# More unread products in TensorE's waits of the first routing, and the first expert's rows ahead of the second routing on VectorE

## The chip, the cores and the metric

The kernel runs on one core of one Trainium2 chip. Its engines run side by side: TensorE multiplies matrices (PE in the profile; PEld is its weight load), VectorE (DVE) and ScalarE (ACT) work element by element, GpSimd (POOL) does small vector work and issues the gathers and scatters, SyncE (SP) issues most other transfers. The metric is the time of one execution on the device in microseconds (us), the median of several runs; lower is better.

## The reference

`x` is the output of an attention layer (a local one and one over means of four positions), 4608 tokens of 512 numbers. Then eight experts share the tokens, each with room for exactly 576:

```python
logits = x @ w_gate                       # 4608 x 8
order = np.argsort(-logits.flatten())     # the best pairs (token, expert) first
for idx in order:
    tok, e = idx // 8, idx % 8
    if assigned[tok] >= 0 or counts[e] >= 576: continue
    assigned[tok] = e; counts[e] += 1
for e in range(8):
    mask = assigned == e
    out[mask] = np.maximum(x[mask] @ w1[e], 0) @ w2[e]   # 512 -> 1024 -> 512
```

## The kernel before, in words

A first part computes attention and the logits (tile `lg`). The second part has eight rounds, one for each expert in the order in which experts fill up.

**Routing (class Routing).** A round finds which expert is full first and at which logit. It looks for the threshold digit by digit, in two halves of the logit's bits (high, then low), three steps each: VectorE compares all keys with a row of thresholds (`cmp`, L802), TensorE counts the hits per expert (L839), VectorE caps the counts (`cs`, L843), TensorE adds them up (L847), VectorE finds the step that is passed (`un`, L854), TensorE hands it to all partitions (L864, L865), and VectorE makes the next thresholds (`thr`, L826). Every step waits for the other engine. Then `emit` ranks the chosen tokens (L1090, L1091) and turns ranks into a list of token numbers, `idx` (one-hot tiles `ohh`, `ohl`, a product of both at L1131, or L1167 in round 0).

**Unread products.** In round 0 TensorE has nothing else to do. `fill(what)` then issues FILL[what] products of a tile of ones (128x256, L789) into a bank `pX` that nobody reads; `rows` does the same with XFILL (L1304) while it waits for the first gathered rows. They stand in TensorE's order like any instruction, ahead of what follows.

**Experts (class Experts).** `weights` loads a round's weights, and `split` cuts each into two fp16 halves, `wh` on ScalarE (L1262) and `wl` on VectorE (L1267, two pieces each). `gather` fetches the token rows (five slices `xg`, GpSimd, L1290). `rows` of round 0 transposes a slice on TensorE (L1313, bank `pX`, two buffers), and ScalarE (L1316) and VectorE (L1318) write its high and low halves to `xt`: these are the row halves of the title. `first` is the first layer, 192 products a round (L1358), which needs slices 0 and 1 for its first columns and 2 to 4 for the rest; `relu` evicts it on ScalarE and VectorE (`ht`, L1386, L1390); `second` is the second layer (L1413, 120 products); `store` scatters the result.

**The order.** Engines execute in the order in which the program issues. Each of these streams has a name and a round, and the table KEYS gives every step of a stream a number; `Plan.run` always issues the step with the smallest number. S is the setup of a routing, R its search and `emit`, W `split`, X `rows`, H `first`, E `relu`, C `second`, L and M the weight loads, G `gather`, Y `store`. S1 and R1 are thus the second routing, which runs beside the layers of the first expert (H0, C0).

Of the kernel before, what the change touches and what calls it, by code (L numbers as in the profile page):

```python
# [6 lines left out]
F32 = mybir.dt.float32  # L7
# [24 lines left out]
NT = NTOK // 128  # L32
# [668 lines left out]
FILL = {"oh": 8, "level": 5, "low": 5, "row": 3, "tot": 4, "rank": 2, "list": 11, "half": 0}  # L701
XFILL = (22, 5, 8)
# [19 lines left out]
class Routing:  # L722
# [37 lines left out]
    def open(self, ctx, ps, ident):  # L760
# [6 lines left out]
        self.zeros = wk.tile([128, 2 * NT], F32, name="zeros")  # L767
        nc.vector.memset(self.zeros, 0.0)
        self.id16 = wk.tile([128, 224], F16, name="id16")
        nc.vector.memset(self.id16[:, 128:], 0.0)  # L770
# [10 lines left out]
        nc.gpsimd.memset(self.ohl[:, NT:], 0.0)  # L781
        nc.scalar.dma_start(self.tri, consts["tri"])
# [33 lines left out]
    def count(self, oh, key, cmp, cap, first, beside=None, tell=None):  # L816
# [5 lines left out]
        for lv, (J, step) in enumerate(LV):  # L822
# [14 lines left out]
            for t in range(0, NT, n):  # L837
                m = min(n, NT - t)
                nc.tensor.matmul(cv[:m * J, :, :m], cmp[:, t:t + m].rearrange("p t j -> p (t j)"), oh[:, :, t:t + m],  # L839
                                 start=t == 0, stop=t + m == NT, skip_group_check=True)  # L840
            yield
# [369 lines left out]
class Experts:  # L1211
# [905 lines left out]
```

## Time and profile before

| what | value |
|---|---|
| median of 3 runs | 707.5 us (703.14, 707.5, 708.33) |
| the profiled execution | 702.79 us |
| its span, first to last instruction | 701.2 us |
| mean granted TensorE clock | 0.972 |

The profile is of one execution; what it has beside its span is 1.6 us. A line of a timeline gives start, duration, engine, source line, operation and names, and in brackets the idle time of the engine just before and what ended it. A granted clock of 1.00 is 2.4 GHz, of 0.50 it is 1.2 GHz.

### The profile page before, as it was taken

Reading aid. Unit: us, or ns where it says so; the run is one execution under the profiler, and the core shown is the slowest. Engines: PE = TensorE matmul, PEld = TensorE weight load, DVE = VectorE, ACT = ScalarE, POOL = GpSimd, SP = SyncE. Lnnn points to the kernel's source line nnn. Section 1 sums busy time; section 2 is a strip of 40 time slices with the busy share of each in tenths; the row PEclk is TensorE's granted clock in tenths of the full one; section 3 lists DMA queues with packets and bytes.
Section 4 is the critical chain, followed back from the end, with each engine's and each line's share of the span. In section 5 each row is a group of like instructions: output and inputs, shape, how many; then the busy total and the mean of one; then the engine's idle time right before and its main releaser. Section 6 shows DMA issues by size and latency. Waiting matters only on the chain.

```text
span 701.2 us, 19377 instructions
## 1 busy us (share of the span) xinstructions
PE 655.7 (94%) x7871; PEld 471.2 (67%) x7871; DVE 485.1 (69%) x1311; ACT 358.0 (51%) x712; POOL 259.5 (37%) x322
## 2 busy tenths in 40 slices
PE   7799989999899878899999899999999999999994
PEld 4678878888888856674675576576574664764741
DVE  5778585778678867799997897896896775510300
ACT  5787977988786723335344453352542454412210
POOL 7678747584684214005131141411501405002011
PEclk9999999999999966999999999999999999999997
DMA  8959888776886615337483661942833976101001
GB/s 241 309 145 234 210 243 245 212 230 197 208 239 181 212 59 180 129 128 230 103 292 101 233 158 44 315 102 70 314 68 123 393 167 164 40 1 62 9 31 38
DMA packets 137714, 116.77 MB, mean 167 GB/s; under 512 B 86232, under 2 KB 114392, under 8 KB 137624
## 3 DMA queue, kind: packets, MB, share of 16 engines
q1 hardware_dynamic: 130104, 93.71, 46.3%
q0 software_dynamic: 6512, 21.24, 9.2%
q8 instruction: 62, 1.02, 0.6%
q10 hardware_dynamic: 1008, 0.58, 0.3%
q14 instruction: 28, 0.23, 0.1%
HBM read 86.00 MB, written 21.23 MB: 153 GB/s over the span
## 4 chain that ended last, share of the span: by engine, by line
PE 46%; DVE 20%; issue 19%; ACT 7%; DMA 4%; POOL 2%; SPq 0%; POOLq 0%; DVEq 0%; ACTq 0%
PE pX L1413 15%; PE pH L1358 12%; PE o L569 3%; DVE wl L1267 2%; PE g L511 2%; POOL out_dram L1437 2%; DVE gtmp L266 2%; PE g L546 2%; PE pR L839 1%; ACT pt L554 1%; DVE ht L1390 1%; PE g L599 1%; DVE cmp L802 1%; PE g L300 1%; DMA nat<-in_q_dram 1%
## 5 line engine op out<-in xcount | busy, mean ns | idle before, releaser
L1358 PE MATMUL pH<-xt,wh 128*128 128x256 f16 (+1 forms) x1024 | 191.0, 286 | 2.6 <-DVE ht L1390 1.9
L1413 PE MATMUL pX<-wh,ht 128*128 128x512 f16 (+1 forms) x640 | 183.0, 379 | 0.0
L1358 PE MATMUL pH<-xt,wl 128*128 128x320 f16 (+1 forms) x512 | 144.7, 287 | 0.0
L1413 PEld LDWEIGHTS <-ht 128*128 128x128 f16 (+1 forms) x960 | 81.6, 100 | 87.3 <-issue 3.0
L1437 POOL DMA_INDIRECT out_dram<-y,idx x40 | 43.8, 1094 | 217.0 <-ACT y L1432 200.0
L1413 PE MATMUL pX<-wl,ht 128*128 128x512 f16 (+1 forms) x320 | 117.9, 380 | 0.0
L1358 PEld LDWEIGHTS <-wh 128*128 128x128 f16 x1024 | 94.6, 98 | 29.1 <-DVE ht L1390 3.0
L1386 ACT ACTIVATE ht<-pH 128x512 f16<-128x512 f32 (+1 forms) x128 | 45.5, 407 | 116.3 <-PE pH L1358 103.1
L1390 DVE SCALAR_TENSOR_TENSOR ht<-pH,ht 128x512 f16<-128x512 f32 (+1 forms) x128 | 52.3, 450 | 60.2 <-ACT ht L1386 60.1
L1267 DVE SCALAR_TENSOR_TENSOR wl<-nat,wh 128x512 f16<-128x512 f32 x128 | 86.7, 686 | 4.5 <-ACT wh L1262 3.9
L1290 POOL DMA_INDIRECT xg<-x_dram,idx x40 | 48.0, 1201 | 72.0 <-DVE idx L1144 37.2
L1432 ACT ACTIVATE y<-pX 128x512 f32<-128x512 f32 (+2 forms) x41 | 23.9, 584 | 93.9 <-PE pX L1413 56.5
L1262 ACT ACTIVATE wh<-nat 128x1024 f16<-128x1024 f32 x64 | 67.0, 1056 | 8.1 <-DMA nat<-in_moe_w_dram 7.3
L1358 PEld LDWEIGHTS <-wl 128*128 128x128 f16 x512 | 50.1, 98 | 12.8
L554 ACT COPY pt<-g 38x512 f32<-38x512 f32 x72 | 41.7, 579 | 17.4 <-PE g L546 15.0
L569 PE MATMUL o<-vw,pt 128*64 128x64 f32 x1152 | 41.6, 224 | 1.8 <-DMA vw<-up_dram 1.7
L536 POOL TENSOR_TENSOR sw<-sw,rs 128x304 f32<-128x304 f32 x36 | 26.3, 734 | 43.1 <-DVE rs L534 24.1
L511 PE MATMUL g<-kt,qz 128*64 128x38 f32 x1152 | 41.1, 225 | 1.1 <-ACT kt L279 1.1
L300 PE MATMUL g<-ident,nat 128*128 128x128 f32 x256 | 37.3, 279 | 4.6 <-DMA nat<-in_k_dram 1.3
L511 PEld LDWEIGHTS g<-kt,qz 128*64 128x64 f32 x1152 | 40.1, 138 | 1.7 <-ACT kt L279 1.2
L569 PEld LDWEIGHTS o<-vw,pt 128*64 128x64 f32 x1152 | 37.1, 138 | 3.9 <-ACT x L581 1.8
L266 POOL TENSOR_TENSOR gtmp<-qz 64x576 f32<-64x576 f32 x28 | 32.0, 1141 | 11.9 <-ACT qz L279 4.2
(227 smaller groups left out, 1135.6 us busy)
## 6 DMA issues: line engine op xcount, KB each, us to landing
nat<-in_moe_w_dram SPq DMA_DIRECT2D x28, 1024.0 KB
vw<-in_v_dram SPq DMA_DIRECT2D x136, 78.0 KB
x_dram<-x SPq DMA_DIRECT2D x36, 256.0 KB
nat<-in_q_dram SPq DMA_DIRECT2D x7, 1024.0 KB
nat<-in_k_dram SPq DMA_DIRECT2D x7, 1024.0 KB
nat<-in_v_dram SPq DMA_DIRECT2D x7, 1024.0 KB
vw<-up_dram SPq DMA_DIRECT2D x36, 64.0 KB
up_dram<-xu SPq DMA_DIRECT2D x8, 256.0 KB
```

The costliest lines, as they stand in the source:

```text
L266: eng.tensor_tensor(tmp.rearrange("p a (w i) -> p a w i", w=NW) if which == "q" else tmp, sv[..., ::2], sv[..., 1::2], op=OP.add)
L511: nc.tensor.matmul(sv[64 * a:64 * a + 64, 4 * g + c], self.qz[b % 2][:, 2 * g + a, w].rearrange("p s q -> p (s q)"), self.kt[b][:, 2 * g + ...
L554: nc.scalar.copy(out[r, :, :, a], p[r].rearrange("p (i h q) -> p i h q", h=4, q=QW))
L569: nc.tensor.matmul(o[64 * i:64 * i + 64, 64 * (4 * g + h):64 * (4 * g + h) + 64], pt[:, 2 * g + i, h].rearrange("p b q -> p (b q)"), self. ...
L1262: nc.scalar.activation(hi, r, AF.Copy, scale=sc)
L1267: nc.vector.scalar_tensor_tensor(lo[:, a:a + LOP], r[:, a:a + LOP], sc, hi[:, a:a + LOP], op0=OP.mult, op1=OP.subtract)
L1290: self.fetched = self.nc.gpsimd.indirect_dma_start(out=xg[:n], out_offset=None, in_=self.x, in_offset=bass.IndirectOffsetOnAxis(ap=idx[:n, ...
L1358: nc.tensor.matmul(p[:, s, :s1 - s0], self.w[k, d][a][:, 128 * f:128 * f + 128], self.xt[k][:, b, d, s0:s1], start=j == 0, stop=j == len(s ...
L1386: nc.scalar.activation(hi, q, AF.Relu)
L1390: nc.vector.scalar_tensor_tensor(lo, q, 0.0, hi, op0=OP.max, op1=OP.subtract)
L1413: nc.tensor.matmul(p[o:o + m], self.ht[k][:, f, h0:h0 + m], self.w[k, 4 + f // 2][b][:, 512 * (f % 2):512 * (f % 2) + 512], start=j < part ...
L1437: i = nc.gpsimd.indirect_dma_start(out=self.out, in_=y[:n], in_offset=None, out_offset=bass.IndirectOffsetOnAxis(ap=plan.vals["idx", k][:n ...
```

## The change

FILL and XFILL are larger, there is one more place with unread products ("kept", four of them, behind the first count of the low half), two tiles are cleared on GpSimd instead of VectorE (`zeros` also later and at another address), and the numbers of rounds 0 and 1 in KEYS are new. All names of an engine's order below come from the program itself; line numbers of the changed kernel are two higher from L843 on.

```diff
-FILL = {"oh": 8, "level": 5, "low": 5, "row": 3, "tot": 4, "rank": 2, "list": 11, "half": 0}
-XFILL = (22, 5, 8)
+FILL = {"oh": 18, "level": 8, "low": 7, "kept": 4, "row": 3, "tot": 4, "rank": 2, "list": 18, "half": 0}
+XFILL = (32, 6, 8)
...
-        self.zeros = wk.tile([128, 2 * NT], F32, name="zeros")
-        nc.vector.memset(self.zeros, 0.0)
         self.id16 = wk.tile([128, 224], F16, name="id16")
-        nc.vector.memset(self.id16[:, 128:], 0.0)
+        nc.gpsimd.memset(self.id16[:, 128:], 0.0)
...
+        self.zeros = wk.tile([128, 2 * NT], F32, name="zeros")
+        nc.gpsimd.memset(self.zeros, 0.0)
...
+            if beside and not lv:
+                self.fill("kept")
...
-    "X0": [70, 72, 76, 77, 80, 82, 83, 85, 89, 90, 93, 97, 100, 102, 105, 106],
+    "X0": [69, 70, 71, 73, 75, 76, 79, 80, 81, 84, 85, 86, 92, 93, 94, 95],
```

On VectorE, between the token list of round 0 and the first capped count of the second routing, before (`eq`, `u`, `am`, `amu`, `oh` and the two big `cmp` are S1; the numbers in names are of tiles):

```order
L1267 SCALAR_TENSOR_TENSOR wl_5257<-nat,wh_5256 128x512
L1318 SCALAR_TENSOR_TENSOR xt<-pX,xt 128x4x128
L948 TENSOR_REDUCE am<-eq 128x36
L950 SCALAR_TENSOR_TENSOR amu<-asg,am 128x36
L951 TENSOR_TENSOR oh<-eq,amu 128x288
L1318 SCALAR_TENSOR_TENSOR xt<-pX,xt 128x4x128
L802 TENSOR_TENSOR cmp_5332<-xh,first 128x2304
L1318 SCALAR_TENSOR_TENSOR xt<-pX,xt 128x4x128
L802 TENSOR_TENSOR cmp_5364<-xl,first 128x2304
L1318 SCALAR_TENSOR_TENSOR xt<-pX,xt 128x4x128
L843 TENSOR_SCALAR cs<-pR 128x16
```

The same place on VectorE in the changed kernel, where the five row halves begin:

```order
L1320 SCALAR_TENSOR_TENSOR xt<-pX,xt 128x4x128
L1269 SCALAR_TENSOR_TENSOR wl_5292<-nat,wh_5291 128x512 x2
L1320 SCALAR_TENSOR_TENSOR xt<-pX,xt 128x4x128 x2
L935 TENSOR_TENSOR eq<-lg,m 128x288
L1320 SCALAR_TENSOR_TENSOR xt<-pX,xt 128x4x128
L937 TENSOR_TENSOR eq<-eq,codes 128x288
L939 TENSOR_SCALAR u<-s 128x36
L1320 SCALAR_TENSOR_TENSOR xt<-pX,xt 128x4x64
L950 TENSOR_REDUCE am<-eq 128x36
```

and further on, up to that capped count:

```order
L802 TENSOR_TENSOR cmp_5443<-xh,first 128x2304
L802 TENSOR_TENSOR cmp_5457<-xl,first 128x2304
L1392 SCALAR_TENSOR_TENSOR ht<-pH,ht 128x512
L1392 SCALAR_TENSOR_TENSOR ht<-pH,ht 128x64
L1269 SCALAR_TENSOR_TENSOR wl_5463<-nat,wh_5462 128x512
L845 TENSOR_SCALAR cs<-pR 128x16
```

The row halves moved ahead of the setup, and one eviction and one weight piece moved ahead of `cs`. The last place is VectorE behind the ranking of the second routing. Before, it goes from the ranking's last use to the one-hot tile and the setup of the third routing so:

```order
L1072 TENSOR_TENSOR used<-used,code 128x1
L1390 SCALAR_TENSOR_TENSOR ht<-pH,ht 128x512
L1390 SCALAR_TENSOR_TENSOR ht<-pH,ht 128x64
L1127 TENSOR_TENSOR ohl<-pl,io 128x1152
L923 TENSOR_REDUCE m<-lg 128x36
```

In the changed kernel the last eviction stands ahead of the scan `at`, and a piece of the second expert's weights ahead of `ohl`; the rows here are the beginning and the end of that stretch:

```order
L1062 TENSOR_TENSOR rem<-cl,pR 128x8
L1392 SCALAR_TENSOR_TENSOR ht<-pH,ht 128x512
L1392 SCALAR_TENSOR_TENSOR ht<-pH,ht 128x64
L1103 SCALAR_TENSOR_TENSOR at<-pR,zeros 128x72
L1105 TENSOR_TENSOR rank<-at,pR 128x72
```

```order
L1074 TENSOR_TENSOR used<-used,code 128x1
L1269 SCALAR_TENSOR_TENSOR wl_5910<-nat,wh_5909 128x512
L1129 TENSOR_TENSOR ohl<-pl,io 128x1152
L1137 COPY odd<-pR 32x36
L1139 TENSOR_TENSOR sm<-pR,odd 32x36
```

On TensorE the order from the first row slice to the third routing's first count is, in counted pieces (T4 the four transposes of a slice, F unread products, H first layer, C second layer, "count" the 18 counting products): before F22 T4 F5 T4 F8 T4 H12 T4 H6, count, ... with 168 more H up to the ranking and behind it, then H30 C12, L1131, C36, count; after F32 T4 F6 T4 H12 F8 T4 H6 T4 H6 T4 H24, count, ... with 144 more H, ranking, C24, L1131, C24, count.

## Rows read from the trace of the kernel before

**Rows 1.** The page: busy time by engine; granted TensorE clock in 40 slices; one costly group

```profile
PE 655.7 (94%) x7871; PEld 471.2 (67%) x7871; DVE 485.1 (69%) x1311; ACT 358.0 (51%) x712; POOL 259.5 (37%) x322
...
PEclk9999999999999966999999999999999999999997
...
L1390 DVE SCALAR_TENSOR_TENSOR ht<-pH,ht 128x512 f16<-128x512 f32 (+1 forms) x128 | 52.3, 450 | 60.2 <-ACT ht L1386 60.1
```

**Rows 2.** Windows: stretch, its length, busy by engine, clock, DMA; behind the second routing

```profile
330.00:690.00 360.00, 356.12 (x2861) 225.04 (x2860) 234.26 (x655) 134.28 (x259) 80.08 (x76) 1.00 0.45 138
```

**Rows 3.** Windows of 2 us in the first routing and behind it

```profile
248.00:250.00 2.00, 1.05 (x20) 0.88 (x18) 1.86 (x10) 1.17 (x2) 1.32 (x9) 0.82 0.41 102
...
264.00:266.00 2.00, 2.00 (x14) 1.24 (x14) 1.59 (x11) 0.12 (x1) 0.24 (x1) 0.50 0.00 0
...
276.00:278.00 2.00, 1.74 (x13) 0.96 (x11) 1.97 (x6) 1.30 (x3) 1.70 (x2) 0.85 0.61 154
...
284.00:286.00 2.00, 2.00 (x11) 1.67 (x10) 2.00 (x4) 0.60 (x1) 0.00 (x0) 0.50 1.05 379
```

**Rows 4.** Timeline of TensorE in the first routing

```profile
247.70 1.03 PE L789 MATMUL pX<-one 128*128 128x256 bf16 x8 [0.26 <-DVE lg L618]
248.57 0.48 PE L839 MATMUL pR<-oh,nat 128*128 128x16 bf16 x13
...
250.26 0.30 PE L839 MATMUL pR<-oh,nat 128*128 128x16 bf16 x5 [1.21 <-DVE nat L802]
...
253.75 1.23 PE L789 MATMUL pX<-one 128*128 128x256 bf16 x5
254.77 0.56 PE L839 MATMUL pR<-oh,cmp 128*128 128x32 bf16 x9
...
269.28 2.56 PE L1167 MATMUL pR<-ht 128*128 128x36 bf16 x36 [0.75 <-DVE ht L1162]
```

**Rows 5.** Timeline of VectorE: first routing, then setup and search of the second

```profile
247.89 0.12 DVE L768 MEMSET zeros<- 128x72 f32 x1 [0.24 <-DMA x_dram<-x]
...
254.16 0.83 DVE L802 TENSOR_TENSOR cmp<-xh,thr 128x640 bf16<-128x640 int16 x2
...
272.08 0.66 DVE L1144 TENSOR_TENSOR idx<-pR,odd 32x5 int32<-32x5 f32 x4
...
276.58 1.89 DVE L1267 SCALAR_TENSOR_TENSOR wl<-nat,wh 128x512 f16<-128x512 f32 x3
...
282.21 0.68 DVE L1318 SCALAR_TENSOR_TENSOR xt<-pX,xt 128x512 f16<-128x512 f32 x1
282.81 1.35 DVE L802 TENSOR_TENSOR cmp<-xh,first 128x2304 bf16<-128x2304 int16 x1
...
287.02 0.17 DVE L843 TENSOR_SCALAR cs<-pR 128x16 f16<-128x16 f32 x1 [0.40 <-PE pR L839]
...
295.88 0.15 DVE L876 SCALAR_TENSOR_TENSOR val<-pR,thr 128x1 f32<-128x1 f32 x1
```

**Rows 6.** Timeline of TensorE and its weight load: first expert and second routing

```profile
271.66 4.88 PE L1304 MATMUL pH<-one 128*128 128x256 bf16 x22
...
276.62 0.42 PEld L1313 LDWEIGHTS pX<-ident,xg 128*128 128x128 f32 x4 [0.57 <-DMA xg<-x_dram,idx]
...
281.22 0.66 PE L1313 MATMUL pX<-ident,xg 128*128 128x128 f32 x4 [1.72 <-DVE xt L1318]
...
292.20 0.70 PE L1358 MATMUL pH<-xt,wl 128*128 128x320 f16 x4
...
309.48 0.20 PE L1090 MATMUL pR<-f,one 128*128 128x72 bf16 x1
...
313.32 0.38 PE L1413 MATMUL pX<-wh,ht 128*128 128x512 f16 x1
...
316.19 0.76 PE L1131 MATMUL pR<-r,ohl 128*128 128x72 bf16 x18
...
324.55 0.60 PE L839 MATMUL pR<-oh,cmp 128*128 128x16 bf16 x18
```

26 rows, old and new, of the table KEYS are left out of this document.

## The prediction

> **What bounds the kernel now.** I read the page first. TensorE is busy 94% of the span, VectorE 69%, and the granted clock is full but for two slices in the middle [rows 1]. The share is an average over stages, so I read windows next. From 330 to 690 us TensorE works 356.12 of 360 us at full clock [rows 2]: whatever comes late or early there is only moved, and about 4 us of idle time is all that could take up a shift. The change acts where that isn't so, in the first routing and in the start of the second. There TensorE and VectorE hand work to each other, and two things are to be seen. The clock: in the window from 248 to 250 us the mean is 0.82, so it fell at about 249.3; it is 0.50 (1.2 GHz instead of 2.4) in the middle of the routing, and 0.85 from 276 to 278, so it rose at about 276.6; it falls once more around 284 to 286 [rows 3]. And the chain: I followed it in the timelines, from the token list of round 0 (`idx`, from 272.08 to 272.74 us) [rows 5] to the first count of the third routing at 324.55 [rows 6]. Behind that count the order of TensorE is the same in both kernels and dense, so the change is worth what it moves that count.
>
> The sum is made against the profiled execution, 702.79 us. It is 4.7 below the median, at the low end of the three runs. One per cent, 7.1 us, is about what a measurement of this kernel can tell from no change.
>
> **The change, first routing, up to `idx`.** An unread product costs 0.109 us at full clock (8 of them from 247.70 to the count's start at 248.57) and 0.204 at half (5 from 253.75 to 254.77) [rows 4]. A level has cover for some of them: the products start at 253.75 and the count behind them needs the second half of `cmp`, which ends at 254.99 [rows 4, 5], about 1.25 us. Five products at half clock take 1.02 and are hidden. Eight take 1.63 at half clock and 0.87 at full.
>
> - At half clock, four levels give 4 x (1.63 - 1.25), and the products of the levels' later waits and the queue behind them bring this to an estimated 0.6 a level, 2.4 in all. Seven instead of five in "low" (+0.4), four in "kept" (4 x 0.204 = 0.8) and seven more in "list" (about half of 1.4 covered, +0.7) come on top. With 0.3 off for the start (below) this is +4.0.
> - At full clock all of these are covered, as 8 products are by 1.25 us. What is gained is in the real work: the 36 products at L1167 take 2.56 us at half clock [rows 4], where 18 of the same kind (72 wide) took 0.76 at full [rows 6], so 36 take about 1.5: -1.1. Four levels of shorter counts and additions give 0.15 each, -0.6. VectorE no longer clears `zeros` and `id` at the start, where it waited 0.24 for a transfer and worked 0.12 [rows 5]: -0.3, between 0 and -0.46. GpSimd does it now and nobody there waits for it. Together -2.0.
> - The ten products more in "oh" take 10 x 0.109 = 1.1 us at full clock; behind the first part of the count TensorE waits 1.21 us for VectorE's comparison, so they are hidden [rows 4]. At half clock up to 0.8 of them would be seen, which I leave to the slow case's range.
>
> Which clock? In the trace of before it fell while eight products were being issued, and the stage ahead of them is not changed. I take the middle case: held by the 18 products at the start, lost once, and back during the long runs in "list" and XFILL. That is -1.0, a bit nearer the gain than the middle, between -2.0 and +4.0.
>
> The Trainium skill (TensorE: Matmul & The Clock Gate, Part 1: The HAM clock gate) says that the throttled clock is the default, that sustained work lifts it and idleness brings it back; by it alone the added products keep the clock, and the sum would start from the gain above. This trace agrees for the rise at 276.6 and not for 264 to 266, where TensorE is busy all of 2.00 us at 0.50.
>
> XFILL's 32 products instead of 22 take 3.5 us at full clock and 6.5 at half. In the trace 22 took 4.88, from 271.66 to 276.54, and the weight load then shows 0.57 us idle until the gathered rows came, at 276.6 [rows 6]. At full clock they are hidden; at half they put the first transposes 1.6 us back. This belongs to the cases above.
>
> **The change, row halves and second routing, counted from `idx`.** All times here are where the end of `idx` stays at 272.74.
>
> Step 1, what is gained. `eq`, `am`, `amu` and `oh` leave the row halves' way, so VectorE finishes the low half of the second slice at about 281.4 instead of 282.89 [rows 5]. The first layer starts earlier, the wait of 1.72 us before the third slice's transposes [rows 6] falls, and so does the time at half clock around 285 [rows 3].
>
> Step 2, what is lost. The third slice's transposes now stand behind eight more first-layer products and eight unread ones on TensorE (16 x 0.109 = 1.75). So they run at 283.2, and VectorE, which has no setup left to do in between, waits about 3 us for them, to 284.4. Then come the low halves of slices 2, 3 and 4 (the last has half the width), with `eq` and its two small steps between them, 2.5, to 286.9; `am`, `amu`, `oh`, 1.1, to 288.0; two `cmp` of 1.3 [rows 5], to 290.5; the pair of evictions, 2 x 52.3 / 128 = 0.8 [rows 1], and one piece of `wl`, 1.89 / 3 = 0.6 [rows 5], which now stand ahead of `cs`; so `cs` comes at 291.9 instead of 287.02 [rows 5], 4.9 later.
>
> Step 3, how much of this reaches TensorE. TensorE has first-layer work of its own meanwhile: the 48 products that ended at 292.9 [rows 6] end at about 289.7, a lead of 2.9 with rounding. But the search takes its 8.86 us from `cs` to `val` (287.02 to 295.88 [rows 5]) with TensorE's products between, so `val` comes at 300.5 to 300.8. Before, ranking followed `val` by 13.6 us (309.48 [rows 6]); it is then at about 314.3. All first-layer products are done by about the time at which TensorE started the second layer before, 313.32 [rows 6], plus 1.0. The lead is gone.
>
> Step 4, the list of the second routing. Before, 30 products of the first layer and 12 of the second (6.5 us) covered VectorE's way from ranking to the one-hot tile at 316.19. Now 24 of the second layer stand there. One costs 0.21: 36 of them lie between 316.95, where the 18 products that began at 316.19 end, and 324.55 [rows 6], 7.6 / 36. So 24 take 5.1, while VectorE's way is longer by an eviction pair (0.8) and a `wl` piece (0.6), which stand ahead of `at` and `ohl`. TensorE waits 1.5 to 2.7 us at L1131. The 24 behind it take 5.1 instead of 7.6 and hide less of the third setup, where TensorE waits about 1.2 more.
>
> Together: the third routing's first count is 4.8 later by these steps. The bounds are +5.0 where no part of it is regained, and +2.4, half of 4.8, where TensorE keeps about that much of its lead of 2.9 through the search. Idle time behind 330 us can take up about 0.5. I take +4.3, nearer the upper end, since the two waits at the end depend on VectorE, and VectorE is late by the whole 4.9.
>
> **Sum.** 702.8 - 1.0 + 4.3 = 706.1, and 706 is the forecast.
>
> **The rivals.** *The clock holds and TensorE's lead stays: faster.* The first routing gives -2.0. Between 276.6 and 294 us TensorE is the partner that waits, and with its idle time (1.72 at one place alone [rows 6]) and the time at half clock around 285 [rows 3] gone, I put the second part at -4 (an estimate: step 1 without steps 3 and 4). 702.8 - 6.0 = 696.8. For it: both waits are in the trace, and the clock at the start was close to holding. Against it: steps 2 to 4, in which VectorE, not TensorE, is what ends last. By the rule of the Trainium skill named above this would be the outcome of the first part.
>
> *The added products run at half clock ahead of every count: slower.* The clock falls at about 249.3 as before, for the work ahead of it is the same, and each of the 35 added products costs 0.204 where its cover is used up. The first part is +4.0, the second +4.3: 702.8 + 8.3 = 711.1; from the median, 715.8. It decides from the point at which the clock is 0.50 while the levels run. For it: before, the clock fell with such products being issued and stayed down when TensorE was busy throughout [rows 3]. Against it: there are more than twice as many at the start.
>
> *The change does nothing in the first routing:* cover hides all products at either clock, and the second part alone is left, 707. This is in the forecast's own range.
>
> **How the numbers follow.** The forecast has 0.46, its own range being 702 to 710.5, since a profiled execution 4.7 below the median says that the same kernel scatters by that much. The faster case has 0.32 and the slower one 0.22. Two thirds of each pass the bound of 7.1 us against the median (696.8 and 715.8 are 10.7 and 8.3 away, less where the profiled execution's luck was no luck). So faster is 0.21, slower 0.15, and the same 0.64. The range takes in most of both: 697 to 715.
>
> **What the profile after would show.** The windows from 248 to 277 us have a clock of 1.00 at first, then one stretch at 0.50; all at 1.00 speaks for the faster case, all at 0.50 from 249.3 for the slower. `idx` comes about 1 us earlier. VectorE waits about 3 us ahead of the third low half, and `cs` comes 4.9 us later, counted from `idx`. TensorE waits for VectorE at the products of the one-hot tiles of the second routing, and its count for the third routing begins 4.3 later, again from `idx`. The forecast is wrong if `cs` isn't late, or if TensorE is ahead of VectorE at the ranking.

## The result, and the profile after

The changed kernel takes 715.93 us (median of 6 runs, 711.85 to 720.6), the kernel before 707.52 beside it (6 runs, 703.14 to 709.35). The ratio is 1.0102, with an interval of 1.0067 to 1.0137: slower by about one per cent (8.4 us between the medians), where 706 was forecast and 715 was the end of the range. The profiled execution took 716.77 us, its span is 715.1.

The page of the changed kernel, busy time by engine and the granted clock, against [rows 1]: TensorE has 7 us more to do, VectorE no more than before, and the two weak slices of the clock are now three weaker dips.

```profile
PE 662.8 (93%) x7917; PEld 476.7 (67%) x7917; DVE 484.9 (68%) x1309; ACT 357.8 (50%) x712; POOL 258.5 (36%) x324
...
PEclk9999999999999988899999999999999999999998
```

The span is 13.9 longer, and not all of that is the change. Steps between fixed points of both traces tell where it lies. The points are the end of the last `lg`, the end of `idx` of round 0, the first `cs` of the second routing, `val`, the ranking at L1090, the product at L1131 and the first count of the third routing; they are read from the timelines of this section and of rows 4 to 6. The last `lg`, before and then after:

```profile
247.48 0.17 DVE L618 TENSOR_REDUCE lg<-g 128x8 f32<-128x16 f32 x1 [0.18 <-PE g L614]
```

```profile
250.54 0.17 DVE L618 TENSOR_REDUCE lg<-g 128x8 f32<-128x16 f32 x1 [0.18 <-PE g L614]
```

| step | before, us | after, us | difference |
|---|---|---|---|
| start to the end of `lg` | 247.65 | 250.71 | +3.06 |
| `lg` to `idx` (first routing) | 25.09 | 26.28 | +1.19 |
| `idx` to `cs` | 14.28 | 22.02 | +7.74 |
| `cs` to `val` | 8.86 | 8.16 | -0.70 |
| `val` to ranking | 13.60 | 13.88 | +0.28 |
| ranking to L1131 (after: L1133) | 6.71 | 7.91 | +1.20 |
| L1131 to the third count | 8.36 | 7.64 | -0.72 |
| third count to the end | 376.65 | 378.50 | +1.85 |

The first line is code that the change doesn't touch. Over the 20 traces of this study that point lies between 246.42 and 254.47 us, whichever the kernel, and the last line between 376.59 and 378.82. So a trace is read here from the end of `lg` to the third count: 76.90 before, 85.89 after, +9.0.

The granted clock, windows of 2 us of the changed kernel (stretch, length, busy by engine, clock, DMA), against [rows 3]:

```profile
250.00:252.00 2.00, 1.56 (x14) 1.10 (x15) 1.65 (x11) 0.76 (x3) 1.29 (x9) 0.70 0.08 18
252.00:254.00 2.00, 2.00 (x11) 1.40 (x10) 0.85 (x4) 1.45 (x3) 1.40 (x5) 0.50 0.34 88
...
256.00:258.00 2.00, 1.55 (x22) 1.03 (x20) 1.63 (x6) 0.42 (x1) 0.00 (x0) 1.00 0.05 20
...
284.00:286.00 2.00, 0.56 (x5) 0.31 (x4) 1.70 (x3) 0.00 (x0) 1.83 (x3) 0.74 0.66 186
286.00:288.00 2.00, 2.00 (x11) 1.44 (x10) 0.00 (x0) 0.00 (x0) 0.00 (x0) 0.50 0.76 262
...
290.00:292.00 2.00, 2.00 (x12) 1.68 (x11) 1.16 (x2) 0.60 (x1) 0.00 (x0) 0.56 1.01 371
...
330.00:332.00 2.00, 2.00 (x6) 0.74 (x5) 1.86 (x8) 0.00 (x0) 0.13 (x1) 0.50 1.03 386
```

The clock fell just as the 18 products at the start began, came back at about 254.2 (the window from 254 to 256 has 0.94) and was full for the levels up to 267.9, which it had not been before. It was at half from there to 271.3, at the end of the first routing. It fell once more at about 285, in a wait of TensorE of 1.44 us for the second slice's low half, and came back near 291.8. A last fall, not seen before, lasts from 329.3 to 332.7 and stands behind the wait at L1133 shown below.

TensorE in the first routing, timeline, against [rows 4]:

```profile
250.77 3.79 PE L789 MATMUL pX<-one 128*128 128x256 bf16 x18 [0.27 <-DVE lg L618]
...
254.40 0.60 PE L839 MATMUL pR<-oh,nat 128*128 128x16 bf16 x18
...
258.15 1.03 PE L789 MATMUL pX<-one 128*128 128x256 bf16 x8
...
259.10 0.60 PE L839 MATMUL pR<-oh,cmp 128*128 128x32 bf16 x9
...
273.54 2.56 PE L1169 MATMUL pR<-ht 128*128 128x36 bf16 x36 [0.65 <-DVE ht L1164]
```

The 18 products took 3.6 us until the first count could start, 0.20 each, as at half clock before. Eight products in a level took 0.95, and the 36 products at L1169 took 2.56 at full clock, exactly as long as at half [rows 4].

The first capped count before came 2.96 us behind the logits:

```profile
250.61 0.17 DVE L843 TENSOR_SCALAR cs<-pR 128x16 f16<-128x16 f32 x1 [0.32 <-PE pR L839]
```

VectorE after, timeline, against [rows 5]:

```profile
255.04 0.17 DVE L845 TENSOR_SCALAR cs<-pR 128x16 f16<-128x16 f32 x1 [2.15 <-PE pR L839]
...
276.34 0.65 DVE L1146 TENSOR_TENSOR idx<-pR,odd 32x5 int32<-32x5 f32 x4
...
285.01 0.68 DVE L1320 SCALAR_TENSOR_TENSOR xt<-pX,xt 128x512 f16<-128x512 f32 x1
...
290.84 0.69 DVE L1320 SCALAR_TENSOR_TENSOR xt<-pX,xt 128x512 f16<-128x512 f32 x1 [5.15 <-ACT xt L1318]
...
297.68 0.82 DVE L1392 SCALAR_TENSOR_TENSOR ht<-pH,ht 128x512 f16<-128x512 f32 x2
298.41 0.68 DVE L1269 SCALAR_TENSOR_TENSOR wl<-nat,wh 128x512 f16<-128x512 f32 x1
...
299.01 0.17 DVE L845 TENSOR_SCALAR cs<-pR 128x16 f16<-128x16 f32 x1
...
307.17 0.16 DVE L878 SCALAR_TENSOR_TENSOR val<-pR,thr 128x1 f32<-128x1 f32 x1
```

VectorE waits 2.15 us for the first count and 5.15 us, instead of the 3 forecast, for the third slice. TensorE's side of that wait, and the two places behind it, against [rows 6]:

```profile
285.75 1.01 PE L1360 MATMUL pH<-xt,wh 128*128 128x256 f16 x4 [1.44 <-DVE xt L1320]
286.56 1.06 PE L1360 MATMUL pH<-xt,wl 128*128 128x256 f16 x4
287.41 1.91 PE L1306 MATMUL pH<-one 128*128 128x256 bf16 x8
289.12 1.06 PE L1315 MATMUL pX<-ident,xg 128*128 128x128 f32 x4
...
321.05 0.20 PE L1092 MATMUL pR<-f,one 128*128 128x72 bf16 x1
...
328.96 0.98 PE L1133 MATMUL pR<-r,ohl 128*128 128x72 bf16 x18 [2.48 <-DVE ohl L1129]
...
336.60 0.62 PE L839 MATMUL pR<-oh,cmp 128*128 128x16 bf16 x18
```

The eight first-layer products, the eight unread ones and the transposes stand in the order forecast, but at half clock: 3.4 us from 285.75 to 289.12 for what sixteen products at 0.109 would do in 1.75.

### The profile page after: what moved, and what is told of

It is laid out like the page before. It is cut to its first block, busy times and chain, and to the rows that moved or that the text cites. A ratio compares the mean times of both kernels' runs of the same rounds, so it can differ in the third digit from the quotient of the medians.

```text
span 715.1 us, 19467 instructions
## 1 busy us (share of the span) xinstructions
PE 662.8 (93%) x7917; PEld 476.7 (67%) x7917; DVE 484.9 (68%) x1309; ACT 357.8 (50%) x712; POOL 258.5 (36%) x324
## 4 chain that ended last, share of the span: by engine, by line
PE 43%; issue 19%; DVE 19%; DMA 8%; ACT 6%; POOL 3%; SPq 2%; POOLq 0%; DVEq 0%; ACTq 0%
PE pX L1415 14%; PE pH L1360 12%; PE o L569 3%; DMA vw<-up_dram 3%; DVE wl L1269 2%; PE pR L839 2%; DVE cmp L802 2%; POOL out_dram L1439 2%; DVE ht L1392 2%; PE g L511 1%; DMA x_dram<-x 1%; PE g L546 1%; DVE gtmp L266 1%; ACT pt L554 1%; PE g L300 1%
## 5 line engine op out<-in xcount | busy, mean ns | idle before, releaser
L1292 POOL DMA_INDIRECT xg<-x_dram,idx x40 | 46.4, 1160 | 72.8 <-issue 34.7
```

The source lines that it names most:

```text
L1292: self.fetched = self.nc.gpsimd.indirect_dma_start(out=xg[:n], out_offset=None, in_=self.x, in_offset=bass.IndirectOffsetOnAxis(ap=idx[:n, ...
```

## The experiments

A ratio stands against runs of the kernel before on the same chip, and single ratios carry about 0.3 to 0.6 per cent either way. The trace tells more, so the steps of every kernel come first (us, as in the table above). The column on the clock says whether it was full or half in the levels of the first routing, and then what it did behind `idx`, between 280 and 290 us.

| kernel | `lg` to `idx` | `idx` to `cs` | `cs` to third count | sum | clock in levels, behind `idx` | ratio |
|---|---|---|---|---|---|---|
| before | 25.09 | 14.28 | 37.53 | 76.90 | half, falls | 1 |
| c2_before | 25.08 | 14.23 | 37.56 | 76.87 | half, falls | 1.002 (0.9993 to 1.0046) |
| after | 26.28 | 22.02 | 37.59 | 85.89 | full, falls | 1.0102 (1.0067 to 1.0137) |
| c1_after | 26.14 | 20.86 | 37.32 | 84.32 | full but the last, falls | 1.0077 (1.0045 to 1.0109) |
| e1_keys | 25.07 | 20.56 | 37.34 | 82.97 | half, falls | 1.0124 (1.0061 to 1.0187) |
| e2_fill | 25.55 | 13.82 | 36.59 | 75.96 | full, full | 1.0075 (1.0026 to 1.0124) |
| e3_nomid | 28.64 | 20.11 | 37.73 | 86.48 | half, falls | 1.0142 (1.0109 to 1.0175) |
| e4_hold | 27.92 | 19.18 | 37.78 | 84.88 | half, full | 1.0155 (1.0122 to 1.0188) |
| e5_t2first | 24.59 | 17.78 | 37.34 | 79.71 | full, full | 1.0079 (1.0043 to 1.0115) |
| e6_csfirst | 24.58 | 17.84 | 39.24 | 81.66 | full, full | 1.0116 (1.0065 to 1.0167) |
| e7_before_hold | 25.03 | 13.83 | 36.60 | 75.46 | half, full | 0.9927 (0.9897 to 0.9956) |
| e8_keys_hold | 25.07 | 19.18 | 37.37 | 81.62 | half, full | 1.0072 (1.0039 to 1.0105) |
| e9_fill | 26.17 | 13.82 | 36.58 | 76.57 | full, dips early | 1.002 (0.9991 to 1.0049) |
| e10_xfill | 25.07 | 13.81 | 36.60 | 75.48 | half, full | 0.9996 (0.9961 to 1.0031) |
| e11_fill_hold | 26.19 | 13.84 | 36.59 | 76.62 | full, full | 1.0035 (0.9997 to 1.0072) |
| e12_both_holds | 25.06 | 13.82 | 36.62 | 75.50 | half, full | 0.9993 (0.9963 to 1.0022) |
| e13_repaired | 25.10 | 16.99 | 39.26 | 81.35 | half, full | 1.0101 (1.0064 to 1.0138) |
| e14_clears | 24.60 | 14.46 | 37.54 | 76.60 | half, falls | 0.9963 (0.9931 to 0.9995) |
| e15_fill_noclears | 27.70 | 13.83 | 36.61 | 78.14 | half, dips early | 1.000 (0.9973 to 1.0026) |
| e16_hold_clears | 24.58 | 13.82 | 36.61 | 75.01 | half, full | 1.0008 (0.9975 to 1.0041) |

**The two halves of the change apart (e1_keys, e2_fill).** The first has the new numbers in KEYS with the rest of the kernel before; the second has the rest of the change with the old numbers.

```diff
 # e1_keys, against the kernel before: the 14 changed rows of KEYS only
-    "X0": [70, 72, 76, 77, 80, 82, 83, 85, 89, ...],
+    "X0": [69, 70, 71, 73, 75, 76, 79, 80, 81, ...],
 # e2_fill, against the changed kernel: the same rows put back
```

> The new order of rounds 0 and 1 alone, with the numbers of unread products and the two cleared tiles as before. Main theory (order and clock): the loss is in the second routing, from the token list idx to its first capped count cs (before 14.3 us from the end of idx, after 22.0); most of it stays here: cs 19 to 22 us behind idx, the first routing as before (25 us from the logits to idx), ratio 1.006 to 1.010. Rival (products): the added unread products cost the time; then cs is 14 to 16 us behind idx and the ratio is 0.998 to 1.003.

> The added unread products and the two moved clears alone, with the order of before. Main theory: the first routing is 1.2 us longer (the 18 products at the start are at half clock and stand ahead of the first count), the clock behind them is full and gives nothing back, since VectorE sets the length of a level; cs stays 14 to 15 us behind idx; ratio 1.000 to 1.003. Rival (products): 1.006 to 1.011. Rival of the prediction (clock pays): 0.996 to 0.998.

The long way from `idx` to `cs` comes with the order alone (20.56) and not with the products (13.82). The ratio of e1_keys, 1.0124, is above the 1.006 to 1.010 expected, with an interval that reaches down to 1.0061. The ratio of e2_fill, 1.0075, is in the range of the rival that blamed the products, though its trace is 0.9 better than the kernel before: five runs between 702.66 and 712.48. In e9_fill, the same without the larger XFILL, twelve runs give 1.002. The traced execution of e2_fill had a full clock through nearly all of the first routing; what the products cost at half clock shows in e3_nomid and e4_hold.

**The wait inside the new order (e3_nomid, e4_hold).** One takes away the eight unread products ahead of the third slice, the other adds 13 where TensorE waits 1.44 us. Where such products fill a wait and the clock stays at 1.00 behind it, this is called a hold below.

```diff
 # e3_nomid, against the changed kernel
-XFILL = (32, 6, 8)
+XFILL = (32, 6, 0)
 # e4_hold, against the changed kernel, in first() ahead of each product
+                    for _ in range(13 if k == f == s == 0 and j == 4 else 0):
+                        nc.tensor.matmul(self.ph[0, 1][:, 0, :256], self.one, ..., start=True, stop=True)
```

> The changed kernel without the eight unread products ahead of the third slice's transposes. Both theories have these products on VectorE's way. Main theory (they run at half clock, 1.7 to 1.9 us): the transposes and cs are 1.7 us earlier, ratio 1.0075. Rival (order alone, cover elsewhere): cs moves by less than 0.5, ratio 1.010.

> The changed kernel with 13 more unread products where TensorE waits 1.4 us for the low half of the second slice, between the first four and the next eight products of the first layer. Main theory (the clock falls in that wait and makes VectorE's wait longer): the clock stays 1.00 to 290 us, the third slice's transposes start about 10.5 instead of 12.1 us behind idx, cs 2 to 2.5 us earlier, ratio 1.007. Rival (the order alone): the clock may hold, but cs is earlier by at most 0.5, ratio 1.010; or the products only push the transposes back, ratio 1.011.

Timeline of TensorE in e4_hold: products of a place in the first routing, then the wait filled and the same products behind it:

```profile
257.63 1.65 PE L789 MATMUL pX<-one 128*128 128x256 bf16 x7
...
283.10 1.58 PE L1361 MATMUL pH<-one 128*128 128x256 bf16 x13
284.70 0.60 PE L1362 MATMUL pH<-xt,wh 128*128 128x256 f16 x4
285.13 0.60 PE L1362 MATMUL pH<-xt,wl 128*128 128x256 f16 x4
285.57 1.04 PE L1306 MATMUL pH<-one 128*128 128x256 bf16 x8
286.44 0.60 PE L1315 MATMUL pX<-ident,xg 128*128 128x128 f32 x4
```

and VectorE there, a capped count of a level and the wait for the third slice:

```profile
256.85 0.19 DVE L845 TENSOR_SCALAR cs<-pR 128x32 f16<-128x32 f32 x1 [0.91 <-PE pR L839]
...
287.71 0.69 DVE L1320 SCALAR_TENSOR_TENSOR xt<-pX,xt 128x512 f16<-128x512 f32 x1 [3.06 <-ACT xt L1318]
```

The clock stays at 1.00, the way from the second slice's products to the transposes is 1.74 instead of 3.37, the wait is 3.06, near the 3 forecast, instead of 5.15, and `cs` comes 19.18 behind `idx` instead of 22.02: the clock is 2.84 of the loss in this trace, in which it was at half for 6.8 us. In c1_after and e1_keys it was at half for 3.4 us; they are 1.7 and 1.4 above 19.18. In e3_nomid the clock fell all the same; without the eight products `cs` came at 20.11, 1.9 below the changed kernel's trace, and 0.75 below that of c1_after. Neither ratio is better, and the traces give a reason: in both, the levels of the first routing ran at half clock but for the first of them, and then eight products a level are in the way of the counts. Seven products of "low" took 1.65 us there, and VectorE waited 0.91 for a count of a level.

From the first `cs` to the ranking these two need 17.07 us, where the old numbers need 14.8 at half clock (before, e1_keys, e8_keys_hold) and the new ones 14.65 at full (after 14.66, e2_fill 14.65). So the added products of the levels, of "low" and of "kept" together cost 2.3 us at half clock, and a full clock saves 0.2.

**Places within the new order (c1_after, e5_t2first, e6_csfirst), and the same hold in the kernel before (e7_before_hold).**

```diff
 # e5_t2first, against the changed kernel: the third slice's transposes ahead of H0
-    "X0": [69, 70, 71, 73, 75, 76, 79, 80, 81, ...],
+    "X0": [69, 70, 71, 73, 75, 76, 76.2, 76.4, 81, ...],
 # e6_csfirst, against the changed kernel: the first capped count ahead of E0 and W0
-    "R1": [109, 111, 114, ...],
+    "R1": [105.2, 105.4, 105.6, ...],
 # e7_before_hold, against the kernel before
-XFILL = (22, 5, 8)
+XFILL = (22, 5, 22)
```

> The changed kernel once more, beside the others of this series. What both theories expect is that it repeats: ratio 1.007 to 1.014, the token list to the first capped count of the second routing 19 to 22 us (19 where the clock is full in 283 to 290 us, 22 where it is half), first routing 25 to 30 us, longer where the clock is half while its levels run.

> The changed kernel with the third slice's transposes (and the eight unread products ahead of them) before the first twelve products of the first layer, as in the kernel before; VectorE's order is untouched. Theory one (TensorE's order makes VectorE wait for the third slice): its low half is written 9 to 10 us behind idx instead of 12 to 14, VectorE's wait of 3 to 5 us is gone, cs comes 15.5 to 17.5 us behind idx, ratio 1.003 to 1.006. Rival (VectorE's own order: the setup behind the row halves and two pieces ahead of cs): VectorE's wait moves to the fourth slice, cs at 18.5 or later, ratio 1.009 or more.

> The changed kernel with the first capped count ahead of the eviction pair and the weight piece on VectorE. Theory one: these two cost cs 1.4 us, so cs comes 1.4 us earlier (17.8 at full clock, 20.6 where the clock falls), and the ratio falls by 0.001 to 0.002, since only part of it stays to the third routing. Rival (the search is bound by TensorE, which has work of its own there): cs earlier, the ranking at the same time, ratio unchanged.

> The kernel before with 22 instead of 8 unread products ahead of the third slice's transposes, where TensorE waits 1.7 us. Clock theory: the clock stays full from 277 us on, idx to cs is 13.8 instead of 14.3 us (as where the clock did not fall), the third routing's count 0.4 to 0.9 earlier, ratio 0.998 to 1.000. Rival (the products only stand in the way, at half clock if the first routing ended at half): the transposes 0.5 to 1.5 late, ratio 1.001 to 1.003.

The changed kernel repeats (1.0077), with the clock falling a little later and for half as long, and 20.86 to `cs`. With the third slice first, VectorE's wait moves to the fourth slice, as the rival had it, and shrinks to 1.67 us; `cs` comes at 17.78, between what the two theories said, and the ratio, 1.0079, is no better. With the count first, `cs` is 1.34 earlier than at a held clock (17.84 against 19.18), but this is of no use to TensorE: its addition of the capped counts (L849) stands behind six products of the first layer, which wait for the eviction pair in this order as in the other. Timeline of TensorE in e6_csfirst, the first of these products, behind the count:

```profile
291.07 0.39 PE L1360 MATMUL pH<-xt,wh 128*128 128x256 f16 x2 [1.15 <-DVE ht L1392]
```

e8_keys_hold, with the old place of `cs`, has nearly the same wait, 1.08. So `cs` to `val` grows from 8.14 to 9.55 and takes the gain back, as the rival had it. The hold in the kernel before gives `idx` to `cs` 13.83 and `cs` to the third count 36.60. That is 1.4 less together than the kernel before, more than the 0.4 to 0.9 expected, without moving the transposes (8.5 behind `idx` in both). Timeline of TensorE there:

```profile
281.83 2.57 PE L1304 MATMUL pH<-one 128*128 128x256 bf16 x22
284.50 0.66 PE L1313 MATMUL pX<-ident,xg 128*128 128x128 f32 x4
```

Its ratio of 0.9927 is the best of the study and better than either theory's; e12_both_holds and e16_hold_clears say what it is worth.

**The order at a held clock, and the products one by one (e8_keys_hold, e9_fill, e10_xfill, e11_fill_hold).**

```diff
 # e8_keys_hold: e1_keys with the 13 products of e4_hold
 # e9_fill: e2_fill with XFILL = (22, 5, 8)
 # e10_xfill, against the kernel before
-XFILL = (22, 5, 8)
+XFILL = (32, 6, 8)
 # e11_fill_hold: e2_fill with XFILL = (32, 6, 22)
```

> The new order with the unread products of before, and 13 more where TensorE waits for the second slice's low half, so that the clock holds there. Beside the kernel before with 14 more at the same wait (ratio 0.993, 13.8 us from idx to cs) this is the price of the order alone at full clock. Theory (the order costs by itself, the clock on top): idx to cs 17.8 to 19.2 us, ratio 1.000 to 1.004. Rival (all of the loss is the clock): cs 15 us or less, ratio 0.993 to 0.997.

> The kernel before with the larger numbers of products in the first routing, the four kept ones and the moved clears; XFILL as before. Theory (each added product is paid at half clock, nothing is gained at full): from the logits to idx 25.3 to 25.6 us where the clock holds and 28 to 29 where it falls, so a scatter of 3 us and more between runs, ratio 1.001 to 1.005. Rival (they are hidden or pay back): ratio 0.996 to 1.000.

> The kernel before with XFILL 32, 6, 8 alone. Theory: ten more products end before the gathered rows come when the clock is full and up to 1.6 us after them when it is half, but they bring the clock back earlier: idx to cs 13.8 to 15.5 us, ratio 0.996 to 1.003. Rival (they stand in the way): 15.5 us or more, ratio 1.003 or more.

> The kernel before with all added products and 14 more ahead of the third slice's transposes. Theory (the hold is worth 0.7%, the products of the first routing cost 0.1 to 0.5%): ratio 0.994 to 0.999, above that of the hold alone. Rival (the products keep the clock through both and add up with the hold): 0.988 to 0.992.

Four windows from the end of `idx` to `cs`, in this order of kernels: before, e7_before_hold, e8_keys_hold, after (stretch, length, PE, PEld, DVE, ACT, POOL busy, clock).

```profile
272.74:287.02 14.28, 11.67 (x85) 8.67 (x84) 13.62 (x31) 6.77 (x11) 7.87 (x7) 0.75 0.67 212
```

```profile
276.00:289.83 13.83, 11.88 (x107) 9.41 (x106) 13.56 (x33) 6.38 (x11) 7.88 (x7) 0.93 0.67 212
```

```profile
275.02:294.20 19.18, 15.89 (x135) 12.31 (x134) 15.38 (x36) 9.56 (x18) 7.36 (x7) 0.93 0.55 176
```

```profile
276.99:299.01 22.02, 16.86 (x129) 12.99 (x128) 15.49 (x35) 9.31 (x17) 7.34 (x7) 0.84 0.47 153
```

This is the account of the loss. VectorE was already full before: 13.62 of 14.28 us. The new order gives it 1.8 more to do ahead of `cs` (15.38) and lets it stand idle for 3.8 us; in the changed kernel's trace the fall of the clock makes that 6.5. At a held clock the order costs 81.62 - 75.46 = 6.2 us against the old order, also with its clock held; against the kernel before as it runs, 4.7. Of the 6.2, 5.35 lie between `idx` and `cs` (19.18 - 13.83). The rival, that all is the clock, falls; the ratio, 1.0072, is above the theory's 1.000 to 1.004.

The products and clears of the first routing cost about 1.1 us in e9_fill and e11_fill_hold (26.17 and 26.19 against 25.07), all of it in the first count; in both traces the clock fell as the 18 products there began. Their ratios, 1.002 and 1.0035, are not clear of 1, and that of e11_fill_hold is above the 0.994 to 0.999 of the theory, in which the hold was worth 0.7%. XFILL at 32 gives the same 13.81 and 36.60 as the hold, ratio 0.9996: in its trace the clock was full from 273.3 us on, 1.8 behind `idx`.

**What is scatter, what adds up (c2_before, e12_both_holds, e13_repaired).** The first is the kernel before itself.

```diff
 # e12_both_holds, against the kernel before
-XFILL = (22, 5, 8)
+XFILL = (32, 5, 22)
 # e13_repaired: e8_keys_hold with the rows "X0" of e5_t2first and "R1" of e6_csfirst
```

> The kernel before, run as an experiment of its own. It gives the scatter: the ratio should be 0.997 to 1.003. Theory (its own second routing is short of 0.5 us of VectorE's time only where the clock falls there): idx to cs 13.8 us if the clock holds behind 277 us and 14.3 if it falls; logits to the third count 75.5 to 77. Rival (in other executions it loses much more than in the one profiled, which would explain a gain of 0.7% by one hold): 78 us or more.

> The kernel before with 32, 5, 22 unread products instead of 22, 5, 8 in the waits for the gathered rows; the first routing is as before. Theory: both hold the clock, idx to cs 13.8, logits to the third count 75.5; ratio 0.992 to 0.998, no better than one hold. Rival (they add up): 0.985 to 0.991. Rival (ten more are in the way): 1.000 or more.

> The new order with the unread products of before, the 13 that hold the clock, the third slice's transposes ahead of the first layer on TensorE, and the capped count ahead of the eviction pair and weight piece on VectorE. Theory (each is worth 1.4 us of idx to cs, and the rest is VectorE waiting with its setup still to do): 16.2 to 16.8 us, ratio 1.000 to 1.005, still above the kernel before. Rival (the two places are all of it): 14 to 15 us, ratio 0.993 to 0.998.

The kernel before repeats its steps within 0.1 us (76.87) and has a ratio of 1.002. So its steps are not what made 702.79 a low base: in c2_before the same steps stand in a span of 705.3. The two holds together have the trace of one (75.50), as the theory said, with a ratio of 0.9993, above its 0.992 to 0.998. The intervals of e7_before_hold and e12_both_holds do not meet, though their steps are the same; so the 0.7 per cent of the first is not shown to be the hold's. What the traces show of it is 1.4 us, 0.2 per cent.

The repaired order comes to 16.99, not to 14: both places together give 2.2 of `idx` to `cs`, of which 1.9 is lost again behind `cs` (39.26 against 37.37). Neither theory's time came true, 16.2 to 16.8 by the nearer one; the ratio of 1.0101 is no better than without the repair.

**The start of the first routing (e14_clears, e15_fill_noclears).** In e2_fill and e4_hold the clock was full through the first count, and yet the first `cs` came 0.9 us behind the count's end. So products and clears were taken apart.

```diff
 # e14_clears: e2_fill with FILL (and "kept": 0) and XFILL of before
 # e15_fill_noclears, against the kernel before: FILL and "kept" alone
+FILL = {"oh": 18, "level": 8, "low": 7, "kept": 4, "row": 3, "tot": 4, "rank": 2, "list": 18, "half": 0}
```

> The kernel before with the two clears moved to GpSimd and no other change. From the end of the logits to the first capped count it needed 2.96 us. Theory (the products are late, the clears bring a little): 2.6 to 2.7. Rival (the wait for transfers now stands at the capped count, which comes up to 0.9 us after its products): 3.0 to 3.6. Ratio 0.998 to 1.002 by either.

> The kernel before with the added products of the first routing and the clears left on VectorE. Theory (the products stand ahead of the first count and run at half clock): 4.0 to 4.6 us from the logits to the first capped count where the clock falls, 2.9 to 3.2 where it holds. Rival (the moved clears did it): 2.9 to 3.1 at either clock. Ratio 1.000 to 1.004 by the theory, 0.997 to 1.001 by the rival.

The clears alone bring the first `cs` to 2.49 us behind the logits, 0.47 earlier than before, and nothing waits for them; 2.6 to 2.7 was expected. The products alone, at full clock through the first count, give 3.37, outside the ranges of both theories. But the products are not what is late there: the first count ends 2.89 us behind the logits, before it ended at 2.91, and `cs` begins 0.48 behind it instead of 0.05. The same delay is larger in e2_fill and e4_hold (0.90 and 0.93). In the other 17 traces `cs` begins 0.03 to 0.05 behind its count. In these three it begins 0.18 to 0.20 us behind the end of GpSimd's first indirect transfer. VectorE and GpSimd in e2_fill, whose count ended at 250.19:

```profile
251.09 0.18 DVE L845 TENSOR_SCALAR cs<-pR 128x16 f16<-128x16 f32 x1 [1.35 <-PE pR L839]
```

```profile
249.75 1.16 POOL L1282 DMA_INDIRECT y<-x_dram,zero  x1 [0.59 <-POOL zero L1280]
```

In e5_t2first and e6_csfirst, with the same products and clears and the same times up to the count, `cs` ran beside that transfer, 2.66 behind the logits. Why it waits in three traces and not in the others is open, and no run tests it. What the 18 products cost the first count is read from its end. With the clears on GpSimd it ends 2.45 behind the logits with eight products (e14_clears) and 2.62 with 18 at full clock, 0.17 later; with 18 of which most or all are at half clock it ends at 3.80 to 4.29. So they cost time at half clock and nearly none at full, and the moved clears cost none.

Behind its first level e15_fill_noclears is once more at half clock: 17.04 from `cs` to the ranking, as in e3_nomid and e4_hold. The ratio of e14_clears is 0.9963 with an interval that ends at 0.9995; e16_hold_clears, with the same clears, does not repeat it.

**The two edits that shorten the trace together (e16_hold_clears).**

```diff
 # e16_hold_clears: e14_clears with XFILL = (22, 5, 22)
```

> The kernel before with 22 instead of 8 unread products ahead of the third slice's transposes and the two clears on GpSimd. Theory (the traces add up: 1.4 and 0.5 us): logits to the third count 75.0 us, ratio 0.995 to 0.999. Rival (the hold is worth more than its trace shows): 0.989 to 0.994. Rival (nothing measurable): 0.999 to 1.002.

The trace adds up as the theory has it, 75.01, 1.9 us less than the kernel before. The ratio, 1.0008, has no gain in it that can be measured, and its interval does not reach down to that of e7_before_hold. Two intervals of the study lie below 1, those of e7_before_hold and e14_clears; this kernel has both their edits and no gain. So no version is shown to beat the kernel before; e16_hold_clears has the shortest steps of both kernels and all experiments.

## Why the prediction was wrong

- **The base.** 706.1 was made against one profiled execution, 4.7 below the median. The text knew of the scatter and used it for the range alone; had the sum stood on the median, it would have been 710.8. The part of the kernel ahead of the change scatters by 8 us between executions, so the sum belonged on the median.
- **First routing, -1.0 forecast, +1.2 in the trace.** The middle case for the clock came the other way round: it fell in the 18 products that were to hold it and was full in the levels. Two terms failed. The ten products more in "oh", forecast as hidden, ran at half clock with the other eight: VectorE waited 2.15 us for the first count, and that step is 4.33 instead of 2.96 long, +1.4, although the clears took 0.5 off it. At full clock they are hidden but for 0.17, as forecast. And the gain at full clock, -1.1 for L1167 and -0.6 for the levels, is nearly nothing: 36 products took 2.56 at either clock, and a level takes 2.37 instead of 2.40 us, because VectorE's steps set its length: a count ends 0.34 us behind its comparison at half clock [rows 4, 5] and 0.31 at full. In all, a full clock saves 0.2 up to the ranking. The clears gave what was forecast (0.47, with 0.3 between 0 and 0.46). The price of the other added products at half clock was put too high: 2.4 for four levels, 0.4 for "low" and 0.8 for "kept" make 3.6, where e3_nomid, e4_hold and e15_fill_noclears show 2.2 to 2.3 with three of the four levels at half, and the 0.7 for "list" shows in no trace (7.29 to 7.38 from the ranking to `idx` in all 20). The traced execution of the changed kernel escaped this price.
- **Step 1, the time at half clock around 285 "falls".** This is the step that failed most. The low half of the second slice is done 8.7 us behind `idx`, as forecast, but the time at half clock did not go; it moved onto VectorE's way and grew. TensorE waits for the first layer's inputs, as before, the clock falls at about 285, and sixteen products and the transposes, for which VectorE waits, take double. The hold of e4_hold gives 2.84 us as its price in the traced execution, and that of e8_keys_hold 1.4 against e1_keys.
- **Step 2, order and length of the wait.** Right at full clock: 3.06 us of wait, and `cs` 19.18 behind `idx` is 4.9 more than before, as forecast to a tenth. The 14.28 of before holds about 0.45 of half clock itself (13.83 in e7_before_hold).
- **Steps 3 and 4.** Right in the sum: from `cs` to the third count 37.59 against 37.53, where the steps left 0.1 to be regained. In the parts, the search is 0.7 shorter than the 8.86 taken over from before, and the way from ranking to L1131 1.2 longer; TensorE's wait there, 2.48, is within 1.5 to 2.7. The wait forecast ahead of the third count, about 1.2, is 1.47 in c1_after. In the traced execution the half clock behind L1133 fills it: the 24 products take 6.8 instead of 5.1 us, and that step is 0.2 longer than in c1_after (7.64 against 7.41). The discount from 4.8 to 4.3 had no ground: nothing is regained up to the third count, and the rest behind it was no shorter.
- **The sum again with what was measured.** 702.8 + 1.2 + 7.8 = 711.8 on the profiled base, 716.5 on the median; 715.93 was measured. The slower rival named the right size (715.8) by luck: its 4.0 for the first routing and 4.3 behind it were 1.2 and 7.8 in the trace. It put the half clock into the levels, where it is found in some executions (e3_nomid, e4_hold), and not into the wait for the third slice.
- **The faster rival** and the rule of the Trainium skill beside it (TensorE: Matmul & The Clock Gate, Part 1: The HAM clock gate), that sustained work lifts the clock: the trace after agrees with it for 256 to 264 us, at 1.00. It brought no time, since TensorE was not what the levels waited for. Where it would have counted, the eighteen products did not keep the clock up in the traces of after, c1_after, e3_nomid, e9_fill and e11_fill_hold, five of ten that have them.

What stays open: why e7_before_hold was 0.7 per cent faster and e12_both_holds and e16_hold_clears, with equal or shorter steps, were not; why the ratios of e2_fill and e1_keys, which are the parts, add up to more than the whole; and what holds up the first `cs` in three traces. The first two are smaller than the scatter of the stage ahead of the change. The steps are those of one execution of each kernel; which clock the other executions had at which step is not on record.

## What to carry to other kernels

Before moving work ahead on an engine, add up its busy time in the window that ends at the step to be reached: VectorE had 13.62 of 14.28 us filled, so moving its work about could gain little there, and an order that opened a wait had to lose. Unread products for the clock paid here only where TensorE is what the stage waits for and where a wait covers them; the 14 of e7_before_hold fit into such a wait and took 1.4 us from the steps behind in the trace, too little for the medians to show, while 18 ahead of a count cost 1.4 where they ran at half clock. And a stretch at half clock does not vanish with the wait in which it was seen: look for the next wait of TensorE ahead of work that another engine needs.

## What was not expected of the hardware

- The 36 products of 36 columns at L1167 take 2.56 us at a clock of 0.50 and at 1.00, 0.07 each. What sets their pace was not tried.
- Eighteen products back to back at the start of the first routing met the fall of the clock in five of ten traces (3.6 us for them in the changed kernel's) and ran at full clock in the other five (2.0 us in e5_t2first, from 247.66 to the count at 249.62).
- The unchanged first part ends anywhere between 246.42 and 254.47 us in 20 traces, nearly as much as the whole loss of 9 us behind it, while single steps behind it mostly repeat within 0.1 us where the clock does the same.
